# Two x row tiles loaded as partition halves on two queues, a shorter warm-up, and half columns in the first matmuls of a two-layer MLP

## The chip, the cores and the metric

The kernel runs on one core of a Trainium2 chip. The metric is the device time of one execution in microseconds (us). "Before" took 293.56 us when the prediction was made (median of 3; 293.25 to 294.12). In the profile, PE is TensorE, PEld its weight loads, DVE is VectorE, ACT is ScalarE, SP is SyncE, POOL is GpSimd, and a q behind an engine's name means its instruction queue (here: issuing DMAs). L80 is line 80 of the kernel profiled; line numbers of the changed kernel are a few higher.

## The reference, cut to what matters

```python
B, S, D, F = 1, 2048, 576, 4608          # all bf16
h = einsum("bsd,df->bsf", x, w1) + b1
r = where(h > 0, h, 0)
h = r * r
out = einsum("bsf,fd->bsd", h, w2) + b2
```

## The kernel before

x is cut into four blocks of 512 rows. For block 0 the kernel loads four row tiles (128 x 576), transposes them on TensorE, and copies the transposes out of PSUM. While it waits for x, TensorE runs warm-up matmuls on constants. The contraction length 576 is 4.5 x 128. So the first 512 columns of w1 (`w1n`) are multiplied in full 128-row steps, with the remaining half step loaded apart (`w1n8`). All other columns (`w1_h`, called w_h in the profile) are multiplied in 64-row steps, two at a time on the two halves of the array, in 16 column steps of a lower and an upper half. Nearly all loads are issued by the sync queue, in the order written.

```python
    WARM = [512] * 6 + [256]
    for i, n in enumerate(WARM):
        keep(nc.tensor.matmul(wps[:, 0:n], lhsT=ones[:, 0:P], rhs=ones[:, 0:n], start=True, stop=True))
    # ... (cut)
    load_x(nc.sync, 0)
    load_x(nc.scalar, 1)
    load_x(nc.sync, 2)
    load_x(nc.scalar, 3)
    for k in range(NK):                 # NK = 4
        load_w1n(nc.sync, k)            # 128 x 512
    load_w1n8(nc.sync, 0)               # 64 x 2 x 128
    load_w1n8(nc.sync, 1)
    # ... (cut: four tiles transposed on TensorE, copied by VectorE and ScalarE)
    for (j0, j1) in [(0, 1), (1, 2), (2, 4), (4, 6), (6, 8), (8, 10), (10, 12)]:
        load_w1(nc.sync, 0, j0, j1)     # 64 partitions x 9 x (j1-j0)*128: lower half
        load_w1(nc.sync, 1, j0, j1)     # upper half
    load_xT(1)                          # block 1 of x, transposed by the DMA
    for (j0, j1) in [(12, 14), (14, 16)]:
        load_w1(nc.sync, 0, j0, j1)
        load_w1(nc.sync, 1, j0, j1)
    # ... (cut: b2, w2, block 2 of x)
    a_full(0, "k_outer")                # w1n columns of block 0:
    #       for k in range(NK):
    #           for g in range(G): full(g, k, k == 0, False)      # 128 x 512 each
    #           if k == 1: make_b1T()
    a_rows(0, 12, 1)                    # the 16 column steps ("rows") of block 0
```

Of the kernel before, what the change touches and what calls it, by code (L numbers as in the profile page):

```python
# [17 lines left out]
def kernel(  # L18
# [9 lines left out]
    nc = tc.nc  # L28
    keep = tc.keep_in_program_order
    P = 128  # L30
    H = 64
    x2 = x.flatten_outer_dims()
# [5 lines left out]
    NK = NC // 2  # L38
    G = 4
# [4 lines left out]
    SB = 512  # L44
# [11 lines left out]

    wps = ps_o.tile([P, 512], FP32, name="wps", tag="po")
    ones = nc.const_aps.tensor(1.0, [P, 512], BF16)
    WARM = [512] * 6 + [256]
    for i, n in enumerate(WARM):  # L60
        keep(nc.tensor.matmul(wps[:, 0:n], lhsT=ones[:, 0:P], rhs=ones[:, 0:n], start=True, stop=True))  # L61

    xs = const.tile([P, RT, D], BF16, name="x_sb")
    w1n = wpool.tile([P, NK, GW], BF16, name="w1n")
    w1n8 = wpool.tile([P, G // 2, P], BF16, name="w1n8")
    w1_h = wpool.tile([P, NC, FH], BF16, name="w1_h")
    w1_v = w1.rearrange("(c p) f -> p c f", p=H)

    def load_x(eng, rt):
        keep(eng.dma_start(out=xs[:, rt, :], in_=x2[rt * P:(rt + 1) * P, :]))  # L70
# [9 lines left out]
        keep(eng.dma_start(out=w1_h[h * H:(h + 1) * H, :, j0 * P:j1 * P],  # L80
                      in_=w1_v[:, :, GW + h * FH + j0 * P:GW + h * FH + j1 * P]))

    load_x(nc.sync, 0)
    load_x(nc.scalar, 1)
    load_x(nc.sync, 2)
    load_x(nc.scalar, 3)
    for k in range(NK):
        load_w1n(nc.sync, k)
    load_w1n8(nc.sync, 0)
# [10 lines left out]
    E3, O, SPC, E = 0, 1, 5, 6  # L100
# [48 lines left out]
    def make_b1T():  # L149
        b1T_ps = ps_o.tile([P, P], BF16, name="b1T_ps", tag="po")  # L150
        keep(nc.tensor.transpose(b1T_ps[:], b1_rows[:], ident[:]))  # L151
        keep(nc.vector.tensor_copy(out=b1T[:], in_=b1T_ps[:, 0:NFT]))
# [6 lines left out]
    def evac_h(sb, bank, ft):  # L159
        r = rpool.tile([P, SB], BF16, name="r", tag="r")  # L160
        keep(nc.scalar.activation(out=r[:], in_=bank[:], func=ACT.Relu, bias=b1T[:, ft:ft + 1], scale=1.0))  # L161
        keep(nc.vector.tensor_tensor(out=hTs[sb][:, ft, :], in0=r[:], in1=r[:], op=ALU.mult))  # L162
# [17 lines left out]
    def a_full(sb, order):  # L180
        xT = xT_blk[sb]
        banks = []
        for g in range(G):
            pool, tag = (ps_o, "po") if g < 2 else (ps_h, "ph")
            banks.append(pool.tile([P, SB], FP32, name="pn", tag=tag))

        def pair(i, start, stop):
            keep(nc.tensor.matmul(banks[2 * i][:], lhsT=w1n8[0:H, i, :], rhs=xT[0:H, SPC, :],  # L188
                             start=start, stop=stop))
            keep(nc.tensor.matmul(banks[2 * i + 1][:], lhsT=w1n8[H:P, i, :], rhs=xT[H:P, E3, :],  # L190
                             start=start, stop=stop))

        def full(g, k, start, stop):
            keep(nc.tensor.matmul(banks[g][:], lhsT=w1n[:, k, g * P:(g + 1) * P], rhs=xT[:, O + k, :],  # L194
                             start=start, stop=stop))

        if order == "rows_first":
            for i in (1, 0):
                pair(i, True, False)
            for g in (2, 3, 0, 1):  # L200
                for k in range(NK):
                    full(g, k, False, k == NK - 1)
                evac_h(sb, banks[g], g)
        else:
            if order == "k_outer":
                for k in range(NK):
                    for g in range(G):
                        full(g, k, k == 0, False)
                    if k == 1:
                        make_b1T()  # L210
            else:
                for g in (2, 3, 0, 1):
                    for k in range(NK):
                        full(g, k, k == 0, False)
            for i in (1, 0):
                pair(i, False, True)
                evac_h(sb, banks[2 * i], 2 * i)
                evac_h(sb, banks[2 * i + 1], 2 * i + 1)
# [55 lines left out]

    alloc_hT(0)
    a_full(0, "k_outer")
    a_rows(0, 12, 1)
    alloc_hT(1)
    load_xT(3)
    a_rows(1)  # L280
    a_full(1, "rows_first")
    phase_b(0, hTs[0], dups=(2, 3))
    alloc_hT(2)
    a_full(2, "g_outer")
    a_rows(2)
    phase_b(1, hTs[1])
# [35 lines left out]
```

## Time and profile before

| | before |
|---|---|
| time, median of 3 | 293.56 us |
| TensorE busy | 98% of the span |
| first warm-up matmul to first matmul of block 0 | 0.78 to 5.46 us |
| first w_h load issued | 5.08 us |
| third column step of the rows waits for w_h until | 13.79 us |
| start of the last addition of the output | 287.74 us |

Three lines of the page: the span, the DMA row (tenths of the 16 DMA engines' time in 40 slices of 7.3 us) and the chain that ended last by engine:

```profile
span 291.4 us, 5457 instructions
...
DMA  6999999900000000000000000000000000000000
...
PE 98%; ACT 0%; DVE 0%; issue 0%
```

TensorE is all but full; only the few microseconds at the beginning and the end are not its own work. The timeline of the head shows the order (columns: start in us, duration of the group, engine, line, operation, tiles, count, and in brackets what it idled for before):

```profile
0.74 0.89 ACTq L70 DMA_DIRECT2D x_sb<-in_x_dram  x2
0.74 0.86 SPq L70 DMA_DIRECT2D x_sb<-in_x_dram  x2
0.78 2.93 PE L61 MATMUL wps<-const-bfloat16-1.0 128*128 128x512 bf16 x7 [0.78 <-PEq L306]
1.65 1.85 SPq L73 DMA_DIRECT2D w1n<-in_w_dram  x4
3.53 0.51 PE L138 MATMUL ta<-ident,x_sb 128*128 128x128 bf16 x3
3.68 1.36 SPq L77 DMA_DIRECT2D w1n_89<-in_w_dram  x2
...
5.08 9.13 SPq L80 DMA_DIRECT2D w_h<-in_w_dram  x11
5.46 1.89 PE L194 MATMUL pn<-xTw,w1n 128*128 128x512 bf16 x8 [0.43 <-ACT xTw L144]
...
9.50 0.38 PE L173 MATMUL ph<-xTw,w_h 64*128 64x512 bf16 x1
```

The two queues issue two x loads each in about 0.9 us. The sync queue then needs 1.85 us for four `w1n` loads, waits briefly, spends 1.36 us on the two small `w1n8` loads, and reaches the first w_h load at 5.08. TensorE warms up for 2.93 us, transposes from 3.53, begins block 0 at 5.46 and the rows at 9.5. The seven warm-up matmuls are 0.43 us apart, the eight of block 0 take 1.89 us together, 0.22 apart at the end: the clock was raised in between.

In the same view, weight loads that waited for a DMA:

```profile
13.79 0.09 PEld L175 LDWEIGHTS <-w_h 64*128 64x128 bf16 x1 [0.52 <-DMA w_h<-in_w_dram]
...
33.20 0.09 PEld L175 LDWEIGHTS <-w_h 64*128 64x128 bf16 x1 [0.30 <-DMA w_h<-in_w_dram]
```

At 13.79, the third column step, TensorE really stalls: the matmul before it began at 13.39, and the usual distance is 0.215 us. At 33.20 no matmul is late, but the load came just in time. Busy time in one stretch before the stall and two after it (window, sum, PE, PEld, DVE, ACT, POOL, clock, DMA share, GB/s) tells why w_h is slow to come:

```profile
10.00:12.00 2.00, 2.00 (x22) 0.91 (x20) 1.34 (x4) 2.00 (x5) 0.00 (x0) 1.00 1.14 225
14.00:18.00 4.00, 4.00 (x40) 1.85 (x38) 1.70 (x4) 2.44 (x5) 0.00 (x0) 1.00 1.23 202
18.00:22.00 4.00, 4.00 (x40) 1.75 (x37) 1.70 (x4) 2.65 (x5) 0.00 (x0) 1.00 1.22 200
```

The DMA engines are full at 200 to 225 GB/s. So a w_h load that is issued later also lands later. The one for which TensorE waits at the third step, the sixth, was issued at 8.46 and landed 5.3 us later.

### The profile page before, as it was taken

What the parts mean: (1) busy time and instruction counts of PE and PEld (TensorE: products, weight loads), DVE (VectorE), ACT (ScalarE), POOL (GpSimd) and SP (SyncE); (2) the same over time, 40 slices, a digit from 0 to 9 for tenths busy, and PEclk for the clock granted to TensorE, in tenths of its full rate; (3) what the DMA queues carried; (4) which work ended last, traced back from release to release, by engine and by line L of the source; (5) the groups of instructions that cost most, each with busy time, mean ns of one, the idle gap of its engine ahead of it and who ended that gap; (6) DMA issues with size and microseconds to landing.
All of it is one profiled execution on the core that took longest, in us unless ns stands there. A gap on an engine that the chain in (4) does not pass through costs nothing.

```text
span 291.4 us, 5457 instructions
## 1 busy us (share of the span) xinstructions
PE 286.5 (98%) x2412; PEld 177.5 (61%) x2412; DVE 81.4 (28%) x189; ACT 93.7 (32%) x154; POOL 1.5 (1%) x8
## 2 busy tenths in 40 slices
PE   8999999999999999999999999999999999999994
PEld 4444444444687875444477877444457878777783
DVE  3444544444531011544411110344440111110110
ACT  4666666666400001766620000466660000000000
POOL 2000000000000000000000000000000000000000
PEclk9999999999999999999999999999999999999999
DMA  6999999900000000000000000000000000000000
GB/s 183 201 200 175 233 358 326 158 7 2 0 23 0 23 20 20 2 1 2 2 0 20 23 3 20 20 2 0 2 0 2 20 24 20 23 0 23 20 23 21
DMA packets 27320, 16.05 MB, mean 55 GB/s; under 512 B 11284, under 2 KB 27296, under 8 KB 27296
## 3 DMA queue, kind: packets, MB, share of 16 engines
q1 hardware_dynamic: 26976, 15.39, 23.2%
q8 instruction: 19, 0.31, 0.4%
q10 hardware_dynamic: 288, 0.30, 0.3%
q14 instruction: 5, 0.04, 0.0%
q0 software_dynamic: 32, 0.01, 0.0%
HBM read 11.36 MB, written 2.36 MB: 47 GB/s over the span
## 4 chain that ended last, share of the span: by engine, by line
PE 98%; ACT 0%; DVE 0%; issue 0%
PE po L233 49%; PE ph L173 23%; PE ph L175 20%; PE pn L194 5%; PE wps L61 1%; PE pn L188 1%; ACT xTw L143 0%; ACT xTw L144 0%; DVE o_sb L242 0%; PE pn L190 0%; PE ta L138 0%; PE tb L141 0%; PE tb L142 0%; PE b1T_ps L151 0%
## 5 line engine op out<-in xcount | busy, mean ns | idle before, releaser
L233 PE MATMUL po<-w_sb,hT 128*128 128x288 bf16 x1152 | 141.6, 286 | 0.0
L233 PEld LDWEIGHTS <-hT 128*128 128x128 bf16 x1152 | 112.6, 98 | 29.3 <-issue 0.8
L175 PE MATMUL ph<-xTw,w_h 64*128 64x512 bf16 x576 | 125.0, 376 | 0.0
L173 PE MATMUL ph<-xTw,w_h 64*128 64x512 bf16 x576 | 125.0, 376 | 0.0
L161 ACT ACTIVATE r<-ph,b1T 128x512 bf16<-128x512 f32 x128 | 81.1, 685 | 41.0 <-PE ph L173 20.5
L162 DVE TENSOR_TENSOR hT<-r 128x512 bf16<-128x512 bf16 x144 | 61.2, 425 | 79.3 <-ACT r L161 79.3
L173 PEld LDWEIGHTS <-w_h 64*128 64x128 bf16 x576 | 54.0, 94 | 36.4
L175 PEld LDWEIGHTS <-w_h 64*128 64x128 bf16 x576 | 54.0, 94 | 32.3 <-DMA w_h<-in_w_dram 0.8
L242 DVE TENSOR_TENSOR o_sb<-po,b_bc 128x288 bf16<-128x288 f32 x32 | 13.2, 453 | 122.5 <-PE po L233 122.5
L161 ACT ACTIVATE r<-pn,b1T 128x512 bf16<-128x512 f32 x16 | 10.0, 688 | 80.9 <-PE pn L190 80.1
L194 PE MATMUL pn<-xTw,w1n 128*128 128x512 bf16 x64 | 14.5, 379 | 0.4 <-ACT xTw L144 0.4
L194 PEld LDWEIGHTS <-w1n 128*128 128x128 bf16 x64 | 6.1, 98 | 7.6 <-DMA w1n<-in_w_dram 0.6
L61 PE MATMUL wps<-const-bfloat16-1.0 128*128 128x512 bf16 (+1 forms) x7 | 2.9, 593 | 0.8 <-PEq L306 0.8
L113 DVE COPY xTw<-xTw 64x2048 bf16<-64x2048 bf16 x4 | 2.8, 688 | 0.5 <-ACT xTw L144 0.4
L114 DVE COPY xTw<-xTw 64x2048 bf16<-64x2048 bf16 x4 | 2.8, 688 | 0.1
L188 PE MATMUL pn<-xTw,w1n_89 64*128 64x512 bf16 x8 | 2.4, 380 | 0.0
L190 PE MATMUL pn<-xTw,w1n_89 64*128 64x512 bf16 x8 | 2.4, 380 | 0.0
L139 DVE COPY xTw<-ta 128x384 bf16<-128x384 bf16 x4 | 1.2, 358 | 4.1 <-PE ta L138 4.1
L61 PEld LDWEIGHTS <-const-bfloat16-1.0 128*128 128x128 bf16 x7 | 0.9, 135 | 2.1 <-issue 2.1
L98 ACT ACT_TABLE_LOAD x1 | 1.3, 1283 | 1.7 <-PEq L306 1.7
L143 ACT COPY xTw<-tb 128x128 bf16<-128x128 bf16 x4 | 1.2, 298 | 1.1 <-PE tb L142 1.1
L138 PE MATMUL ta<-ident,x_sb 128*128 128x128 bf16 x12 | 1.4, 240 | 0.0
(20 smaller groups left out, 8.4 us busy)
## 6 DMA issues: line engine op xcount, KB each, us to landing
w_sb<-in_w_dram SPq DMA_DIRECT2D x6, 864.0 KB, 11.5
w_h<-in_w_dram SPq DMA_DIRECT2D x14, 288.0 KB, 6.7
out_dram<-o_sb SPq DMA_DIRECT2D x15, 144.0 KB, 1.8
w_h<-in_w_dram SPq DMA_DIRECT2D x4, 144.0 KB, 3.4
w1n<-in_w_dram SPq DMA_DIRECT2D x4, 128.0 KB, 3.3
x_sb<-in_x_dram ACTq DMA_DIRECT2D x2, 144.0 KB, 3.1
x_sb<-in_x_dram SPq DMA_DIRECT2D x2, 144.0 KB, 2.8
b_bc<-in_b_dram SPq DMA_DIRECT2D x1, 144.0 KB, 6.1
```

Source lines behind the costliest of these rows:

```text
L61: keep(nc.tensor.matmul(wps[:, 0:n], lhsT=ones[:, 0:P], rhs=ones[:, 0:n], start=True, stop=True))
L113: keep(nc.vector.tensor_copy(out=xT[0:H, SPC:SPC + 4, :], in_=xT[H:P, E3:E3 + 4, :]))
L114: keep(nc.vector.tensor_copy(out=xT[H:P, SPC:SPC + 4, :], in_=xT[0:H, O:O + 4, :]))
L161: keep(nc.scalar.activation(out=r[:], in_=bank[:], func=ACT.Relu, bias=b1T[:, ft:ft + 1], scale=1.0))
L162: keep(nc.vector.tensor_tensor(out=hTs[sb][:, ft, :], in0=r[:], in1=r[:], op=ALU.mult))
L173: keep(nc.tensor.matmul(bx[:], lhsT=w1_h[0:H, LO_C[i], jc], rhs=xT[0:H, LO_W[i], :], start=(i == 0), stop=(i == NC - 1)))
L175: keep(nc.tensor.matmul(by[:], lhsT=w1_h[H:P, UP_C[i], jc], rhs=xT[H:P, UP_W[i], :], start=(i == 0), stop=(i == NC - 1)))
L188: keep(nc.tensor.matmul(banks[2 * i][:], lhsT=w1n8[0:H, i, :], rhs=xT[0:H, SPC, :], start=start, stop=stop))
L190: keep(nc.tensor.matmul(banks[2 * i + 1][:], lhsT=w1n8[H:P, i, :], rhs=xT[H:P, E3, :], start=start, stop=stop))
L194: keep(nc.tensor.matmul(banks[g][:], lhsT=w1n[:, k, g * P:(g + 1) * P], rhs=xT[:, O + k, :], start=start, stop=stop))
L233: keep(nc.tensor.matmul(po[h][:, 0:DH], lhsT=hT[:, ft, jj * P:(jj + 1) * P], rhs=w2_sb[:, ft, h * DH:(h + 1) * DH], start=(i == 0), stop=( ...
L242: keep(nc.vector.tensor_tensor(out=o_sb[:, h * DH:(h + 1) * DH], in0=po[h][:, 0:DH], in1=b2_bc[:, h * DH:(h + 1) * DH], op=ALU.add,))
```

## The change

Its intent is to have the first x tiles sooner: each of the first two is cut into two halves of 64 partitions that go down two queues at once. The warm-up is shortened to fit, and the first matmuls of block 0 need only half of the columns, hence only the first two x tiles. The fourth x load also moves from ScalarE's queue to the sync queue.

```diff
-    WARM = [512] * 6 + [256]
+    WARM = [512] * 4 + [256]
...
+    def load_x_half(eng, rt, h):
+        keep(eng.dma_start(out=xs[h * H:(h + 1) * H, rt, :], in_=x2[rt * P + h * H:rt * P + (h + 1) * H, :]))
...
-    load_x(nc.sync, 0)
-    load_x(nc.scalar, 1)
+    for rt in range(2):
+        load_x_half(nc.sync, rt, 0)
+        load_x_half(nc.scalar, rt, 1)
     load_x(nc.sync, 2)
-    load_x(nc.scalar, 3)
+    load_x(nc.sync, 3)
...
             if order == "k_outer":
-                for k in range(NK):
+                for half in range(2):
+                    hc = slice(half * (SB // 2), (half + 1) * (SB // 2))
                     for g in range(G):
-                        full(g, k, k == 0, False)
+                        keep(nc.tensor.matmul(banks[g][:, hc], lhsT=w1n[:, 0, g * P:(g + 1) * P],
+                                              rhs=xT[:, O, hc], start=(half == 0), stop=False))
+                for k in range(1, NK):
+                    for g in range(G):
+                        full(g, k, False, False)
```

## The prediction

> **What bounds the kernel now.** The chain of waits lies 98% on TensorE, busy 286.5 of 291.4 us. The change can only touch the head. In the timeline the seven warm-up matmuls run 0.78 to 3.71 us, one per 0.43; the first x tile releases the transposes at 3.5; VectorE's four copies run 4.07 to 5.31, ScalarE's eight 4.23 to 5.69; block 0's first matmul starts at 5.46, the paired rows (L173/L175) at 9.5. At most about 1 us of 293 could be gained.
>
> The head has a second bound, the weights. The timeline shows two weight loads waiting for a w1 half (w_h): 0.52 us at 13.79 (third column step of the rows, first 288 KB load of the upper half) and 0.30 at 33.20 (twelfth step). At the first, L175 resumes at 13.79 instead of about 13.4. At the second no matmul is late, but no slack is left. From 8 to beyond 30 us the DMA share is near or over 1 at about 200 GB/s: the w1 loads are paced by the transfers, and their start by the sync queue's issue order.
>
> **What the change does.** The x bytes stay. Removed: two warm-up matmuls (0.86 us of filler, ending at about 2.85). Added: eight 256-column matmuls for four of 512 (0 to 0.1 us), and two DMA issues. The sync queue issues four x loads before w1 instead of two. An x issue took 0.38 to 0.42 us there, a w1n issue 0.43; I take a half tile to cost about as much as a whole one. Estimate: sync issues x halves at 0.74 and 1.13, x2 at 1.53, x3 at 1.98, w1n 0 at 2.43 (before: 1.65), the first w_h at 5.6 to 5.7 (before: 5.08; 0.2 us of semaphore wait falls away).
>
> - First x tile: lands 0.2 to 0.4 before its old 3.45 (issue 0.74 plus 2.7).
> - x2, x3: 0.4 to 0.8 later than their 4.1 to 4.35.
> - w1n 0: took 3.4 from issue to landing; now 2.9 to 3.4, landing at 5.3 to 5.8 (before: 5.05). Half columns let four matmuls start without x2 and x3, but they need w1n 0, which now comes last: first matmul at 5.3 to 5.8, no gain, up to 0.3 lost.
> - Rows: the 288 KB load lands 0.4 to 0.6 later, at 14.2 to 14.4. TensorE waits there whatever the head gained; the twelfth step follows with the same shift.
>
> The Trainium skill ("DMA: Bandwidth & Descriptors", Issuing engines are not separate DMA queues) says that issuing from several engines saves only the sequencer's issue time; the trace agrees that issue time (0.4 us each) is what moves here, and on the sync queue it moves the wrong way.
>
> **Clock.** "TensorE: Matmul & The Clock Gate" (Part 1) says the clock is released after a window of about 3.4 us of activity. The trace agrees: warm-up matmuls are 0.43 us apart, block 0's 0.215. A shorter warm-up leaves a gap near 3 us; if the release comes a window later, block 0 runs partly at half rate, up to 1 us more, mostly hidden by the w_h wait.
>
> **Predicted time:** 294.05 us (0.5 more), 8 in 10 between 293.4 and 294.8. Faster by over 2%: 0.003; within 2%: 0.99; slower: 0.007.
>
> **What would show it.** Transposes begin at about 3.2; first L213 matmul at 5.3 to 5.8, released by w1n; first w_h issue at 5.6 or later; the stall in the third step ends at 14.2 to 14.4; after it a constant shift.
>
> **What would make it wrong.** Half-tile issues well under 0.4 us; transfers catching up before 13.8 us; cold matmuls past 7 us; another w_h wait at the twelfth step.

## More of the kernel before

The profiled execution took 293.13 us, so it lies at the fast end of before's own times.

Last, the end of the program:

```profile
287.74 0.46 DVE L242 TENSOR_TENSOR o_sb<-po,b_bc 128x288 bf16<-128x288 f32 x1 [3.95 <-PE po L233]
```

From the start of this last addition to the end of the span are 291.37 - 287.74 = 3.63 us.

## The result, and the profile after

The changed kernel took 294.82 us (median of 6; 294.67 to 295.17) against 293.64 us for before (6 runs). The ratio is 1.0038, with a 95% interval of 1.0024 to 1.0052: about 1.1 us slower. Ratios here and below are the mean time of one kernel's fast runs over that of the other's of the same rounds, so not quite the ratio of the medians quoted. Before itself spread from 293.2 to 295.0 over all its runs, the changed kernel only over 0.5 us.

The page after, its span and its chain by engine:

```profile
span 292.9 us, 5462 instructions
...
PE 93%; SPq 3%; DMA 2%; issue 0%; DVE 0%
```

The chain that ended last now runs through the sync queue and a DMA before TensorE takes over. The timeline of the head, as above:

```profile
0.74 1.19 ACTq L70 DMA_DIRECT2D x_sb<-in_x_dram  x2
0.74 1.46 SPq L70 DMA_DIRECT2D x_sb<-in_x_dram  x2
0.79 2.08 PE L61 MATMUL wps<-const-bfloat16-1.0 128*128 128x512 bf16 x5 [0.79 <-PEq L315]
2.25 1.08 SPq L73 DMA_DIRECT2D x_sb<-in_x_dram  x2
3.37 1.85 SPq L76 DMA_DIRECT2D w1n<-in_w_dram  x4
3.38 0.48 PE L142 MATMUL ta<-ident,x_sb 128*128 128x128 bf16 x3 [0.52 <-DMA x_sb<-in_x_dram]
...
5.27 1.30 SPq L80 DMA_DIRECT2D w1n_87<-in_w_dram  x2
5.50 0.24 PEld L142 LDWEIGHTS <-x_sb 128*128 128x128 bf16 x3 [0.33 <-DMA x_sb<-in_x_dram]
6.16 1.42 PE L213 MATMUL pn<-xTw,w1n 128*128 128x256 bf16 x8
...
6.62 7.97 SPq L83 DMA_DIRECT2D w_h<-in_w_dram  x10
...
10.60 0.38 PE L177 MATMUL ph<-xTw,w_h 64*128 64x512 bf16 x1
```

The four half loads took the sync queue 1.46 us for two and ScalarE's queue 1.19 us for two; the two whole ones after them 1.08 us. The `w1n` loads begin at 3.37 instead of 1.65, and the first w_h load is issued at 6.62 instead of 5.08. TensorE gets its first x tile at 3.38 instead of 3.53, but the fourth only at 5.50, and block 0 begins at 6.16 instead of 5.46. The five warm-up matmuls are followed by transposes as slow as before the release (three of them in 0.48 us), and the clock record in the packed trace has the full clock only from 6.96 us, where before had it from 4.0.

Weight loads that waited for w_h:

```profile
10.89 0.09 PEld L179 LDWEIGHTS <-w_h 64*128 64x128 bf16 x1 [0.41 <-DMA w_h<-in_w_dram]
12.79 0.09 PEld L179 LDWEIGHTS <-w_h 64*128 64x128 bf16 x1 [0.27 <-DMA w_h<-in_w_dram]
15.71 0.09 PEld L179 LDWEIGHTS <-w_h 64*128 64x128 bf16 x1 [1.25 <-DMA w_h<-in_w_dram]
```

The wait at the third column step has grown from 0.52 to 1.25 us and ends at 15.71 instead of 13.79. The chain, in order of time (start, duration, what), shows where that came from:

```profile
0.74 0.58 SPq L70
...
1.39 0.81 SPq L70
...
2.25 0.60 SPq L73
...
10.01 5.66 DMA w_h<-in_w_dram
```

Every step from 0.74 to 10.01 is the sync queue's issuing. The first half tile took 0.58 us, the second 0.81 and the third x load, a whole tile, still 0.60; all x issues before had been 0.38 to 0.46.

The end:

```profile
289.66 0.46 DVE L251 TENSOR_TENSOR o_sb<-po,b_bc 128x288 bf16<-128x288 f32 x1 [3.95 <-PE po L242]
```

The last addition starts 1.92 us later than before, exactly the delay of the third step (15.71 - 13.79). Of these 1.92 us, 1.55 are the later issue of the sixth w_h load (10.01 instead of 8.46); the rest is its longer way from issue to landing (5.66 us instead of 5.29). That rest need not be the change's: in a3 below, which has the old loads, the same load took 5.65. But the span is only 1.5 us longer (and the timed difference is 1.1, since before's profiled execution was a fast one): from the addition to the end are 292.92 - 289.66 = 3.25 us, where they were 3.63. That is a second, unlooked-for effect, which is taken up below.

### The profile page after: what moved, and what is told of

Read it like the earlier page. It is cut to its first block, busy times and chain, and to the rows that moved or that the text cites. A ratio compares the mean times of both kernels' runs of the same rounds, so it can differ in the third digit from the quotient of the medians.

```text
span 292.9 us, 5462 instructions
## 1 busy us (share of the span) xinstructions
PE 287.1 (98%) x2411; PEld 178.2 (61%) x2414; DVE 81.6 (28%) x189; ACT 94.0 (32%) x154; POOL 1.5 (1%) x8
## 4 chain that ended last, share of the span: by engine, by line
PE 93%; SPq 3%; DMA 2%; issue 0%; DVE 0%
PE po L242 48%; PE ph L177 21%; PE ph L179 20%; PE pn L198 3%; DMA w_h<-in_w_dram 2%; SPq L83 1%; SPq L76 1%; SPq L70 0%; SPq L80 0%; PE pn L192 0%; SPq L73 0%; DVE o_sb L251 0%; PE pn L194 0%
## 5 line engine op out<-in xcount | busy, mean ns | idle before, releaser
L179 PE MATMUL ph<-xTw,w_h 64*128 64x512 bf16 x576 | 125.0, 376 | 0.8 <-DMA w_h<-in_w_dram 0.8
L179 PEld LDWEIGHTS <-w_h 64*128 64x128 bf16 x576 | 54.0, 94 | 35.4 <-DMA w_h<-in_w_dram 2.2
L198 PE MATMUL pn<-xTw,w1n 128*128 128x512 bf16 x57 | 13.3, 379 | 0.3 <-issue 0.2
L61 PE MATMUL wps<-const-bfloat16-1.0 128*128 128x512 bf16 (+1 forms) x5 | 2.1, 579 | 0.8 <-PEq L315 0.8
L142 PE MATMUL ta<-ident,x_sb 128*128 128x128 bf16 x12 | 2.0, 302 | 0.7 <-DMA x_sb<-in_x_dram 0.5
L142 PEld LDWEIGHTS <-x_sb 128*128 128x128 bf16 x12 | 1.0, 123 | 2.0 <-DMA x_sb<-in_x_dram 1.9
```

Source lines behind the costliest of these rows:

```text
L142: keep(nc.tensor.transpose(ta[:, i, :], xs[:, j, i * P:(i + 1) * P], ident[:]))
L179: keep(nc.tensor.matmul(by[:], lhsT=w1_h[H:P, UP_C[i], jc], rhs=xT[H:P, UP_W[i], :], start=(i == 0), stop=(i == NC - 1)))
L198: keep(nc.tensor.matmul(banks[g][:], lhsT=w1n[:, k, g * P:(g + 1) * P], rhs=xT[:, O + k, :], start=start, stop=stop))
```

## The experiments

Two theories at the start. **A, issue order:** the new loads hold up the sync queue, w_h is issued late, and TensorE waits for it at the third column step. **B, clock:** the shorter warm-up leaves TensorE at half clock for longer, and that is the loss. A third, **C**, came out of the second set of runs. All runs gave correct results. Each was timed against before in the same rounds. The table has, from each profile, the first w_h issue, when the clock was released, when the last addition of the output began, and the time from there to the end of the span:

| kernel | w_h issue | clock at | last addition | tail | ratio to before (95%) |
|---|---|---|---|---|---|
| before | 5.08 | 4.00 | 287.74 | 3.63 | 1 |
| changed | 6.62 | 6.96 | 289.66 | 3.25 | 1.0038 (1.0024, 1.0052) |
| a5 new loads only | 6.63 | 6.29 | 289.64 | 3.26 | 1.0034 (1.0020, 1.0048) |
| a1 changed, warm-up back | 6.63 | 4.15 | 289.77 | 3.26 | 1.0036 (1.0024, 1.0049) |
| a2 changed, old loads | 5.05 | 8.78 | 289.23 | 3.65 | 1.0007 (0.9991, 1.0023) |
| a3 half columns only | 5.01 | 5.15 | 288.03 | 3.63 | 0.9998 (0.9985, 1.0011) |
| a4 changed, column halves | 5.92 | 9.51 | 289.59 | 3.26 | 1.0017 (0.9997, 1.0036) |
| b3 changed, w1n8 on GpSimd | 5.25 | 9.37 | 289.98 | 3.80 | 1.0054 (1.0039, 1.0069) |
| b5 b3 with warm-up back | 5.26 | 4.85 | 288.54 | 3.80 | 1.0023 (1.0005, 1.0041) |
| a6 short warm-up only | 5.04 | 8.72 | 289.36 | 3.64 | 1.0018 (0.9997, 1.0038) |
| c1 new loads only, column halves | 5.92 | 6.00 | 290.04 | 3.28 | 1.0015 (0.9999, 1.0032) |
| b1 before, w1n8 on GpSimd | 3.63 | 4.49 | 288.57 | 2.98 | 0.9961 (0.9943, 0.9978) |
| b2 b1 with half columns | 3.73 | 6.36 | 287.94 | 2.98 | 0.9946 (0.9929, 0.9962) |
| b4 b2, all w_h loads first | 3.64 | 5.30 | 287.42 | 2.96 | 0.9954 (0.9941, 0.9967) |

A profile is a single execution, and the timed ones differ: the clock's release comes at another moment in each, so the ratio and not the profile's span decides.

### a5: the new loads alone

```diff
 # kernel before, with only the load hunks of the change: load_x_half, and
+    for rt in range(2):
+        load_x_half(nc.sync, rt, 0)
+        load_x_half(nc.scalar, rt, 1)
     load_x(nc.sync, 2)
+    load_x(nc.sync, 3)
```

> The kernel before with the new x loads alone (full warm-up, full columns). Theory A (issue order: half-tile loads keep the sync queue busy longer, the w_h loads start about 1.5 us later, and TensorE waits for the fifth and sixth of them at the third column step): about +1.1 us (0.8 to 1.5), first w_h issue at 6.5 to 6.7, clock released at about 4 us, stall of the third step ending at 15.4 to 15.8. Theory B (the shorter warm-up leaves the clock at half rate for one window more, and that is the loss): at most +0.3 us.

Measured: 294.66 us median, ratio 1.0034, about 1.0 us of the 1.1. Timeline of a5 (sync queue), and its weight load at the third step:

```profile
0.74 1.46 SPq L70 DMA_DIRECT2D x_sb<-in_x_dram  x2
...
6.63 7.95 SPq L83 DMA_DIRECT2D w_h<-in_w_dram  x10
...
15.69 0.09 PEld L179 LDWEIGHTS <-w_h 64*128 64x128 bf16 x1 [1.36 <-DMA w_h<-in_w_dram]
```

The issue times repeat to a hundredth, and the stall ends at 15.69 (15.71 in the changed kernel). The loads alone make nearly the whole loss: A. The clock was released at 6.29, later than A had guessed (about 4), though the warm-up was full; that mattered nothing here.

### a1: the changed kernel with the warm-up back

```diff
-    WARM = [512] * 4 + [256]
+    WARM = [512] * 6 + [256]
```

> The changed kernel with the seven warm-up matmuls back. Theory A: no gain over the changed kernel, +1.0 to +1.3 us against before; clock released at about 4 us, block 0 of TensorE earlier by up to 1 us, all of it spent again waiting at the third column step, whose stall ends at the same 15.4 to 15.8. Theory B: most of the 1.1 us comes back, +0.3 us or less.

Measured: 294.71 us, ratio 1.0036, the clock released at 4.15, and the third step's stall ended at 15.81. Nothing was gained, as A said. Within the changed kernel the clock is hidden behind the wait for w_h. B falls as the explanation of this loss. The same wait would also explain why the changed kernel's times spread so little: whatever the clock does to the head, TensorE ends up waiting for the same load. a5's and a1's times, with that wait too, spread over 0.35 and 0.28 us.

### a2: the changed kernel with the old loads

```diff
-    for rt in range(2):
-        load_x_half(nc.sync, rt, 0)
-        load_x_half(nc.scalar, rt, 1)
+    load_x(nc.sync, 0)
+    load_x(nc.scalar, 1)
     load_x(nc.sync, 2)
-    load_x(nc.sync, 3)
+    load_x(nc.scalar, 3)
```

> The changed kernel with the four whole x loads of before back (short warm-up and half columns stay). Theory A: w_h issue at 5.1 as before; what is left is the clock alone: if it is released near 7 us, rows reach the third step at about 14.4 instead of 13.8, +0.3 to +0.7 us; if it is released near 4, 0 us. Theory B: +1.0 us or more.

Measured: 293.78 us median, with times from 293.23 to 294.64, ratio 1.0007: no loss that is clear of noise. The profile fell in the slowest of them. Its clock was released only at 8.78 and TensorE reached the third step after the w_h load had landed, so no wait was left. B's 1.0 us or more is excluded; A's 0.3 to 0.7 for a late clock is at the upper end of the interval (0.0023 x 293.7 = 0.7 us).

### a3: half columns alone

```diff
 # kernel before, with only the last hunk of the change (half columns for k = 0)
```

> The kernel before with the half columns of the first k alone. First matmul of block 0 at 5.1 to 5.2 instead of 5.46 (it needs w1n 0, landed at 5.05, and two of the four copies). Theory A: the 0.2 to 0.3 us gained are given back at the third column step, whose stall ends at 13.7 to 13.9 as before: -0.1 to +0.1 us. A theory that the head is bound by TensorE alone (A false): -0.2 to -0.4 us.

Measured: 293.61 us, ratio 0.9998. The first matmul came at 5.41 and not at 5.1 to 5.2, because the clock was released at 5.15 and the transposes ran slowly until then. The stall of the third step was still there and ended at 14.08, so a gain in the head could not have shown. The miss leaves the half columns' own worth open; their effect was zero here.

### a4: column halves in place of partition halves

```diff
     def load_x_half(eng, rt, h):
-        keep(eng.dma_start(out=xs[h * H:(h + 1) * H, rt, :], in_=x2[rt * P + h * H:rt * P + (h + 1) * H, :]))
+        keep(eng.dma_start(out=xs[:, rt, h * DH:(h + 1) * DH], in_=x2[rt * P:(rt + 1) * P, h * DH:(h + 1) * DH]))
```

> The changed kernel with the first two x tiles halved along the columns (128 partitions x 288) instead of along the partitions, on the same two queues in the same order. If the long issues (0.54 to 0.81 us a half tile against 0.38 to 0.46 a whole one) come with transfers of 64 partitions: each column half issues in about 0.4 us, the first w_h at 5.6 to 5.8 instead of 6.62, the third step's stall ends at 14.4 to 14.9 instead of 15.7, and the time is 0.2 to 0.7 us over before (0.5 to 0.9 under the changed kernel). If they come with two small loads on two queues, whatever the shape: as the changed kernel, +1.1 us.

Measured: 294.45 us, ratio 1.0017. Timeline of a4, the issues and the first transposes:

```profile
0.74 0.88 SPq L70 DMA_DIRECT2D x_sb<-in_x_dram  x2
0.75 0.90 ACTq L70 DMA_DIRECT2D x_sb<-in_x_dram  x2
1.67 0.90 SPq L73 DMA_DIRECT2D x_sb<-in_x_dram  x2
...
3.00 0.50 PE L142 MATMUL ta<-ident,x_sb 128*128 128x128 bf16 x3
...
5.92 9.49 SPq L83 DMA_DIRECT2D w_h<-in_w_dram  x11
```

Two column halves take 0.88 us on the sync queue where two partition halves took 1.46, and the two whole tiles after them 0.90 where they took 1.08. The first w_h issue moves from 6.62 to 5.92. So it is the partition half, 64 partitions instead of 128 for the same bytes, that is slow to issue, and not the number of loads. The other loads of the head fit: those on 64 partitions (`w1n8`, w_h) took about 0.6 us or more each, those on 128 partitions 0.38 to 0.48, but for the first whole tile behind the halves (0.60). Why that is so no run here shows. The times of the two cuts are less clear than their issues: a4 is 0.6 us under the changed kernel by the ratios, but the intervals overlap. The first transposes began at 3.00, 0.5 us before those of the kernel before: the intent of the change does work with this cut. But a4 was no faster than before. In its profile the clock was released only at 9.51, and no wait for w_h was left.

### c1: column halves alone

```diff
 # a5 with load_x_half as in a4: full warm-up, full columns
```

> The kernel before with the new x loads alone, but halved along the columns. Its twin with partition halves took +1.0 us. Issue order theory: x halves issue in 0.4, first w_h at 5.9 (0.8 after before's, 0.7 ahead of the twin's 6.63), stall of the third step ends at 14.6 to 15.0, +0.3 to +0.8 us against before, 0.3 or more under the twin. If the number of loads and not their issue time counts: +1.0.

Measured: 294.02 us, ratio 1.0015, about 0.4 us over before and about 0.6 under a5: inside what the issue theory expected, though its interval overlaps a5's. Its profile was the slowest of its six executions. Its third step's stall ended at 15.14, a little past the range, and it had one more wait in a later step (L179 going on at 35.52, 1.15 us after the matmul before).

### b3: the sync queue relieved

```diff
-    load_w1n8(nc.sync, 0)
-    load_w1n8(nc.sync, 1)
...
     nc.gpsimd.dma_start(out=b1_rows[0:NFT, :], in_=b1.rearrange("(ft p) -> ft p", p=P))
+    load_w1n8(nc.gpsimd, 0)
+    load_w1n8(nc.gpsimd, 1)
```

> The changed kernel with the two w1n8 loads (1.3 us of the sync queue) issued from GpSimd. Theory A (the sync queue's issue order is what costs): first w_h issue at 5.2 to 5.4, i.e. back at before's 5.08, no stall past 14.2; what is left is the later start of block 0 and the clock's luck: +0.1 to +0.6 us over before, 0.5 or more under the changed kernel. If the sync queue is not the cause: as the changed kernel, +1.1 us.

Measured: 295.55 us, ratio 1.0054. This was a miss. The first w_h issue did come at 5.25 and no wait for w_h was left, as A said, but the kernel was slower still. Timeline of b3 (warm-up, first w_h issue, first matmuls of block 0):

```profile
0.78 2.08 PE L61 MATMUL wps<-const-bfloat16-1.0 128*128 128x512 bf16 x5 [0.78 <-PEq L315]
...
5.25 9.88 SPq L83 DMA_DIRECT2D w_h<-in_w_dram  x11
...
6.89 1.89 PE L213 MATMUL pn<-xTw,w1n 128*128 128x256 bf16 x8 [0.52 <-ACT xTw L148]
```

The eight matmuls on 256 columns need 1.89 us here and needed 1.42 in the changed kernel: they ran at half clock throughout. The release came at 9.37. In the four profiles with five warm-up matmuls so far it had come at 6.96 to 9.51, in the ones with seven at 4.0 to 6.4. Hence theory **C**: the short warm-up, with which TensorE stood idle for 0.46 to 0.98 us between the warm-up and the first tile (in a4 for 0.67 after the second tile), puts the clock's release off, and once w_h is early that is what binds. A sees only the first of two bounds.

### b5: b3 with the warm-up back

```diff
-    WARM = [512] * 4 + [256]
+    WARM = [512] * 6 + [256]
```

> The kernel with the changed loads and half columns, w1n8 from GpSimd, and the seven warm-up matmuls back; its twin with five took +1.6 us although its w_h loads were early. Theory C: clock released at 4 to 6.5, rows at 10.4 to 11.0, +0.2 to +0.8 us against before, so 0.8 or more under the twin. If something else made the twin slow (the late x2 and x3, the loads from GpSimd): +1.3 us or more.

Measured: 294.30 us, ratio 1.0023, 0.9 us under b3 by the ratios (0.0031 x 293.7; the two were timed in different rounds, each against before, and their intervals just touch). Timeline of b5, the same rows:

```profile
0.78 2.93 PE L61 MATMUL wps<-const-bfloat16-1.0 128*128 128x512 bf16 x7 [0.78 <-PEq L315]
...
5.26 9.65 SPq L83 DMA_DIRECT2D w_h<-in_w_dram  x11
...
6.65 1.05 PE L213 MATMUL pn<-xTw,w1n 128*128 128x256 bf16 x8 [0.54 <-DMA w1n<-in_w_dram]
```

With the longer warm-up the eight half-column matmuls take 1.05 us instead of 1.89, the clock is released at 4.85, and the last addition comes 1.44 us earlier than in b3. C holds: the warm-up is the only edit between the two. What remains over before (0.7 us) is the start of block 0: at 6.65, released by `w1n`, instead of 5.46.

### a6: the short warm-up alone

```diff
-    WARM = [512] * 6 + [256]     # kernel before
+    WARM = [512] * 4 + [256]
```

> The kernel before with five warm-up matmuls instead of seven. Theory C, added to A: the shorter warm-up leaves TensorE idle for about 1 us before the first x tile, and the clock is released a window later (7 to 9.5 us in the four profiles with five matmuls, 4 to 6.4 in the five with seven): release at 7 or later, rows at 10.5 to 11.5, no stall at the third step, +0.2 to +0.9 us. If the clock's release only depends on luck: 0 us and a release anywhere from 4 to 7.

Measured: 294.44 us, ratio 1.0018 (interval just touching 1), the clock at 8.72, no stall at the third step, and times from 293.65 to 295.29. All nine profiles with seven warm-up matmuls have their release between 4.0 and 6.4 us, all five with five between 6.9 and 9.6. Where in that range it comes differs from profile to profile. Counted from the first matmul, the release came after 3.2 to 5.6 us in the nine, none of which had a pause of TensorE over 0.2 us before it, and after 6.2 to 8.7 us in the five, which all had one of 0.46 us or more. Whether the pause or the missing matmuls decide was not tested apart. The clock record's stretches of full clock are 283.31, 286.72 or 290.13 us long, that is 83, 84 or 85 times 3.413 us, which fits a clock that changes only at the ends of windows of that length.

### b1, b2, b4: towards a faster kernel

```diff
 # b1: the kernel before with the diff of b3
 # b2: b1 with the half columns of a3
 # b4: b2, and
-    load_xT(1)
     for (j0, j1) in [(12, 14), (14, 16)]:
         load_w1(nc.sync, 0, j0, j1)
         load_w1(nc.sync, 1, j0, j1)
+    load_xT(1)
...
-    a_rows(0, 12, 1)
+    a_rows(0, 14, 1)
```

> The kernel before with the two w1n8 loads issued from GpSimd. Theory A: first w_h issue at 3.5 to 3.7 instead of 5.08, the 288 KB half lands at 12.3 to 12.9, the stall at 13.8 is gone; gain 0.2 us in executions where the clock is released at about 4 us (less where it comes late, since TensorE then comes later than the load): -0.1 to -0.4 us. If the w_h loads don't bound the head: 0.

> The same with the half columns of the changed kernel. They gave 0 alone; with the w_h stall gone their 0.0 to 0.3 us stay: first matmul of block 0 at 5.1 to 5.4, -0.2 to -0.6 us against before, and 0.0 to 0.3 under the kernel with the w1n8 move alone.

> The version with w1n8 from GpSimd and half columns, with the last four w_h loads ahead of the transposing loads of block 1, and the duplication of block 1 two steps later. With w1n8 moved, one profile still showed TensorE waiting 1.0 us at the twelfth step for the w_h load issued behind the transposes. That wait falls away: 0.0 to 0.5 us under that version, -1.2 to -2.0 us against before. If the transposes, now later, hold up VectorE: no gain or a loss.

Measured: b1 292.90 us, ratio 0.9961; b2 292.58, ratio 0.9946; b4 292.48, ratio 0.9954. All three beat both kernels, by 1.1 to 1.6 us against before. Timelines of b1, the first w_h issue, and a later matmul that waited for w_h:

```profile
3.63 11.57 SPq L80 DMA_DIRECT2D w_h<-in_w_dram  x12
...
34.05 0.39 PE L175 MATMUL ph<-xTw,w_h 64*128 64x512 bf16 x1 [0.63 <-DMA w_h<-in_w_dram]
```

It comes 1.45 us earlier than before, and the stall at 13.8 is gone. But the gain was larger than the 0.1 to 0.4 us expected. Part of it is not in the head at all. The span of b1, and its last addition:

```profile
span 291.6 us, 5455 instructions
...
288.57 0.46 DVE L242 TENSOR_TENSOR o_sb<-po,b_bc 128x288 bf16<-128x288 f32 x1 [3.95 <-PE po L233]
```

From the addition to the end are 2.98 us, where before had 3.63. The end turns out to go with how many loads the kernel issues. The DMAs of the two hardware queues use eight semaphores in turn (0 to 7). After the last store the instruction records of the trace have a row of six or seven waits of the sync engine, for these semaphores and a few others, mostly 0.06 to 0.08 us apart, with one pause of about 0.45 us in the row or just before it. The last store takes 1.6 us from issue to landing in all fourteen profiles. What differs is how much of the row is left when it lands:

- semaphore 1 in before, a2, a3 and a6: waited for early, the pause still to come, 0.75 us of row left, tail 3.63 to 3.65; in b3 and b5 the row is one wait longer, 0.91 left, tail 3.80;
- semaphore 3 in the changed kernel, a1, a4, a5 and c1: the pause already over, 0.34 left, tail 3.25 to 3.28;
- semaphore 7 in b1, b2 and b4: the last one waited for, 0.08 left, tail 2.96 to 2.98.

After the row follow 0.82 us in all of them. So the traces show where the time of the end goes; that the count of DMAs on the hardware queues decides it (58 in the first group, 60 in the second, 56 in the third) fits all these kernels, but for the 0.17 us between before and b3, and no run changed it alone. It also closes two sums: the changed kernel lost 1.92 us on TensorE and got 0.4 back at the end, and b3, with the same number of loads on the hardware queues as before, has its slow end (3.80) on top of its slow head.

b4 was to take away the wait at the twelfth step. In b1's profile (the slowest but one of its six, 293.33) TensorE stood from 33.05 to 34.05 for the w_h load that is issued behind the transposing loads; b2's and b4's profiles have no such wait. b4's times (292.13 to 292.88) spread a little less than b2's and b1's (0.75 us against 0.93 and 1.14), but the three can't be told apart: their intervals overlap, and neither b2's nor b4's expected further gain was shown.

## Why the prediction was right or wrong

- **That the kernel gets slower by a fraction of a per cent, for the delay of w_h at the third column step: right.** a5 and a1 show it: the loads alone give 1.0034 and the warm-up changes nothing. The predicted 294.05 was too low: 0.5 us more was forecast, and about 1.1 came. The median of 294.82 lies 0.02 over the range given (up to 294.8); the ratio applied to the time known then gives 1.0038 x 293.56 = 294.68. That it comes so near is partly luck: TensorE lost more than was forecast, and 0.4 us came back at the end of the program, which the prediction did not foresee.
- **"I take a half tile to cost about as much as a whole one": this step failed.** It is the term that was mis-sized. A half tile took 0.54 to 0.81 us to issue against 0.38 to 0.46 for a whole one, and the first whole tile after it 0.60. Sum on the sync queue: the x loads took 1.46 + 1.08 = 2.54 us instead of 0.86, 1.68 more, while about 0.2 of waiting and a little of `w1n8` fell away; so w_h was issued 1.54 later and not 0.5 to 0.6. With column halves, which issue in 0.39 to 0.48, it was 0.84 later (a4, c1). So about 0.84 of the delay is the two more x issues on the sync queue, the fourth whole tile among them, and 0.70 the slow cut. The profile before held a warning: the `w1n8` loads of 64 partitions took 1.36 us for two, though they move a quarter of the bytes of a `w1n` load each.
- **The third step's stall ending at 14.2 to 14.4: wrong in size, in the main for the same reason.** It ended at 15.71; 1.55 of the 1.92 us is the later issue.
- **First x tile 0.2 to 0.4 us earlier: right in sign, a little too much.** The transposes began at 3.38, 0.15 us earlier.
- **First matmul of block 0 at 5.3 to 5.8: wrong, 6.16.** `w1n` was issued at 3.37 and not at 2.43, and the fourth x tile held the transposes up until 5.50; again the issue times.
- **Clock: the mechanism was right, the risk came true, and it was hidden as said.** The release came at 6.96. a1 shows that it costs nothing in the changed kernel; b3 and b5 show that it would cost about 0.9 us as soon as w_h were early. The prediction held a late release to be a possibility; it came in all five profiles with the short warm-up.
- **"After it a constant shift": right on TensorE, wrong at the very end.** The delay of 1.92 us is unchanged at the last addition; 0.4 of it came back in the tail.

The Trainium skill warns against this cut, if for another reason: "DMA: Bandwidth & Descriptors", Rules for kernel authors, advises against two transfers to disjoint partition halves, since both halves run on the same 16 DMA engines, and recommends one transfer of 128 partitions. The runs agree in the outcome (1.0034 for the loads alone), and show a cost the row doesn't name, the issue time. The prediction cited another section of the page and overlooked this row. On the clock, "TensorE: Matmul & The Clock Gate" (Part 1) speaks of an activity window of about 3.4 us that runs freely; the scatter of the release over 2.4 us with an unchanged warm-up (4.0 to 6.4) agrees with a window whose phase the kernel does not control, and so do the steps of 3.413 us in the clock record.

What stays open: why 64-partition loads issue more slowly; what the halves would cost with the fourth x load left on ScalarE's queue, which no run tried; how much activity in a window the clock asks for; how much of the gain of b1, b2 and b4 is the end alone (about 0.65 us, as an estimate from the tails of 3.63 and 2.98); and how often the twelfth step has to wait.

## What to carry to other kernels

When loads are added or cut in the head of a kernel, add up the issue times of the queue that carries them, with durations from the trace for that shape, and follow the last load of the queue to whoever waits for it: here the weights at 13.8 us, not x at 3.5, paid. Splitting a small load cost less issue time along the columns than along the partitions, though neither cut made this kernel faster; what helped here was to take unrelated small loads off the busy queue. When a bound is removed and the time does not follow, look for a second one right behind it (the clock), and check the end of the span before crediting the head.

## What the Trainium skill lacked or had wrong

- "DMA: Bandwidth & Descriptors", Issuing engines are not separate DMA queues, calls the issue time usually small relative to the DMA. Here it set the pace of the head: 0.38 to 0.81 us per load, and 9.3 us (0.74 to 10.01) of the chain that ended last was issuing with its small gaps.
- No page read here has the issue time by shape on this chip: a half tile of 64 partitions took 0.54 to 0.81 us, the same bytes as 128 partitions x 288 columns 0.39 to 0.48, a whole tile 0.38 to 0.46 (0.60 behind two half tiles).
- "TensorE: Matmul & The Clock Gate" (Part 1) gives the release of the clock at about 4 us with 0.5 us either way, and elsewhere in the part calls it run-variable. Here, counted from the first matmul, it scattered from 3.2 to 5.6 us with seven warm-up matmuls and from 6.2 to 8.7 with five, worth about 0.9 us of run time between b3 and b5. A pause of TensorE of 0.46 us or more before the release goes with the later group.
- The same page (Part 4) says that the full clock does not engage for transposes. Here three transposes of the first x tile took 0.51 us before the release and those of the third 0.33, after it, so transposes issued as matmuls against an identity do run faster at the full clock. Whether they are in the mode that the page means, the trace does not show.
- No page read here has the end of a program going with the number of DMAs: 2.96 to 3.80 us from the last addition to the end, in groups by the semaphore of the last store.
